# Turning expert rows in 32x32 squares on VectorE, with four first-layer banks

## The chip, the cores and the metric

The kernel runs on one core of a Trainium2 chip. Its time is device microseconds for one launch: 2286.07 us, the median of 3 runs (2285.0 to 2286.5). One more execution was profiled; it took 2288.12 us, and from its first to its last instruction (the span) 2286.2 us. All times on a trace count from the start of that span. The engines are TensorE (PE, with its weight loads PEld), VectorE (DVE), ScalarE (ACT), GpSimd (POOL) and SyncE (SP, which issues most DMAs).

## The reference

An attention without softmax, whose output goes through a mixture of experts with one expert per token.

```python
# u, v: (8, 2496, 256); z: (8, 2496, 64); f32
attn = np.maximum(z @ z.transpose(0, 2, 1) / 2496, 0.0) ** 2
x = (u * (attn @ v)).reshape(19968, 256)
logits = x @ w_gate + modality_bias[modality_id]        # 8 experts
e_idx = np.argmax(logits, axis=1)
gate = softmax(logits)[token, e_idx]
for e in range(8):                                       # w1: (8, 256, 1024), w2: (8, 1024, 256)
    h = np.maximum(x[mask_e] @ w1[e], 0.0)
    out[mask_e] = gate[mask_e, None] * (h @ w2[e])
```

## The kernel before

Matmuls are exact to f32 by parts: an operand is split into a high part, rounded to the format that PE takes (F32R), and a low part, the remainder. A product is high x high + high x low + low x high. ACT makes the high part by a copy, DVE the low part by a subtraction.

**Attention stage.** For each of 8 batches, 5 chunks of 512 queries go through 10 steps of 256 keys: scores, ReLU and square, split, and the product with v. Beside them DVE evacuates finished chunks, multiplies by u, computes the gate logits of each token (`logits`, L396, in 16 calls per chunk of two instructions of 128x256) and the routing of each batch; POOL scatters every token's row (256 values, gate, token number: 258 words) with an indirect DMA into `xs`, at the next place of its expert (`scatter`, L509). A planner (`beside`, L886) deals these pieces out over the steps by assumed costs and due steps, so it sets the order of DVE and ACT; SP's order in this stage is made by the framework's scheduler. Meanwhile the expert weights are copied to a layout of their own in DRAM, `w1s` and `w2s` (`lay_weights`, L204).

**Expert stage.** The rows of each expert are taken in tiles of 512. Tiles -4 to -1 are of the expert with most tokens so far; they run while the last batch's routing is finished (its late logits, routing, scatters and the plan of all further tiles: the list `between`, L1091 on). Tiles 0 to 34 follow by the plan, and a quarter tile of 128 rows closes (`run_quarter`, L1038). A tile (`run_tile`, L1066) has 8 passes `f`. In each, `up` (L975) makes one group of 6 matmuls over the 256 inputs for 128 hidden units into one PSUM bank `ph`, ACT takes ReLU and the high part `hh` from it, DVE the low part `hl`; two passes later `down` (L992) adds the products with w2 for the tile's four 128-row parts, into four banks `po`. After the last pass `finish` (L1004) multiplies by the gate and scatters the rows to the output. `ph` has two banks (pool `ps_h`), and two more (`ps_m`) serve all that is passing: turned rows, the last chunk's rows, the routing's counts.

The first layer contracts over the 256 inputs, so rows must be turned: inputs to partitions. `fetch` (L747) loads a tile with one DMA, four rows of 258 words per partition. `turn` (L833) has PE turn it with 8 transposes of 128x128 into two banks (`turn_rows`), and ACT and DVE take the high and the low part from there (`part_rows`). A tile turns its successor after pass 1, the tiles before 0 after pass 5; tile -4 is turned five steps before the end of attention (`turn_early`, `part_early`). `prefetch` (L1032) asks for a tile's rows up to two tiles ahead; a tile's weights are asked for two tiles ahead and split in passes 2 to 5 of the preceding tile.

Instructions of an engine run in the order given. A wait holds all behind it on that engine.

Of the kernel before, what the change touches and what calls it, by code (L numbers as in the profile page):

```python
# [9 lines left out]
F32 = mybir.dt.float32  # L10
F32R = mybir.dt.float32r
I32 = mybir.dt.int32
AF = mybir.ActivationFunctionType
ALU = mybir.AluOpType
AX = mybir.AxisListType
P = 128
T = 512
PSUM = bass.MemoryType.PSUM
# [3 lines left out]
def ins_of(x):  # L22
    return getattr(x, "ins", x)
# [3 lines left out]
def tile_attention_moe(ctx: ExitStack, tc: tile.TileContext, u, v, zt, mid, wg, mb, w1, w2, out):  # L27
# [11 lines left out]
    nc = tc.nc  # L39
    B, S, D = u.shape  # L40
# [4 lines left out]
    KD, KF = D // P, F // P  # L45
    J = T // P
# [3 lines left out]
    assert (B - 1) * S >= E * T and D == 2 * P and 2 * DK == P and LAST == T - 64 and F % P == 0  # L50
    NCOL = NCH * J
    XW = D + 2
    CAP = N
    EARLY = min(4, (B - 1) * S // E // T)
    UNC = -(-N // T) - EARLY
# [32 lines left out]
    def bank_tile(shape, name):  # L88
        return bank["pool"].tile(shape, F32, tag=bank["tag"], name=name)
# [113 lines left out]

    def lay_weights(e, n):  # L204
        if n == 0:
            nc.sync.dma_start(out=w1s[e], in_=w1[e].rearrange("(k p) f -> p k f", p=P))
        else:
            nc.sync.dma_start(out=w2s[e], in_=w2[e].rearrange("(j p) d -> p j d", p=P))

# [158 lines left out]
    def take_last_rows(b, c):  # L368
        (parts, x), ut = turned_rows.pop((b, c)), U.pop((b, c))
        for n, y in enumerate(parts):  # L370
            j = slice(n * J // 2, (n + 1) * J // 2)
            nc.vector.tensor_tensor(out=x[:, j, 0:D], in0=y, in1=ut[:, j, :], op=ALU.mult)
        X[b, c] = x
# [292 lines left out]
    def at(g, f, *args):  # L666
        tasks.setdefault(g, []).append((f, args))

    def queue(g, end, *pieces):

        due.setdefault(g, []).append((end, pieces))

    def act(us, f, *args):
        return ("A", us, f, args)

    def dve(us, f, *args):
        return ("D", us, f, args)

    def none(f, *args):
        return (None, 0.0, f, args)  # L680
# [58 lines left out]
    ready, fetched = {"n": 0}, {"n": 0}  # L739
    data = mybir.DependencyInfo(mybir.DependencyClass.Sync, mybir.DependencyReason.DATA)  # L740

    def wait_rows(i):
        for s in scatters[ready["n"]:]:
            tc.add_manual_dep(i, s.name, data, reason="rows of tokens")
        ready["n"] = len(scatters)

    def fetch(t, r0=0, nj=J):  # L747

        n = t + EARLY
        cell = first[0:1, 1:2] if t < 0 else meta[0:1, t, 0:1]  # L750
        row = nc.sync.value_load(cell, min_val=0, max_val=(E - 1) * CAP if t < 0 else E * CAP - T)
        k = fetched["n"] % 3
        fetched["n"] += 1
        xg = head[k // 2].tile([P, J, XW], F32R, tag=f"xg{k}", name="xg")[:, 0:nj, :].bitcast(F32)
        r0 += n * T if t < 0 else 0
        src = xs[bass.ds(row + r0 if r0 else row, nj * P), :]
        i = ins_of(nc.sync.dma_start(out=xg, in_=src.rearrange("(p j) c -> p j c", j=nj)))
        wait_rows(i)
        TL[t] = xg

    def weight_tiles(pool, n):
        W[n] = (
# [47 lines left out]
        if EARLY > 1:  # L810
            fetch(1 - EARLY)

    def turn_rows(t, dh):

        xg = TL[t]
        nj = xg.shape[1]
        pt = bank_tile([P, T], "pt")[:, 0:nj * P]
        for j in range(nj):
            nc.tensor.transpose(  # L819
                out=pt[:, j * P:(j + 1) * P].bitcast(F32R),  # L820
                in_=xg[:, j, dh * P:(dh + 1) * P].bitcast(F32R),
                identity=ident_r,
            )
        return pt

    def part_rows(x, dh, pt):
        nc.scalar.copy(out=x[0][:, dh, :], in_=pt)
        nc.vector.tensor_tensor(out=x[1][:, dh, :], in0=pt, in1=x[0][:, dh, :].bitcast(F32), op=ALU.subtract)

    def turned_tiles(nj):  # L830
        return [turned.tile([P, KD, T], F32R, tag="zm", bufs=NCH + 1, name=n)[:, :, 0:nj * P] for n in ("xh", "xl")]

    def turn(t):  # L833
        x = turned_tiles(TL[t].shape[1])
        for dh in range(KD):
            part_rows(x, dh, turn_rows(t, dh))
        TL[t] = (TL[t], *x)

    first_turned = []

    def turn_early(t):
        first_turned[:] = [turn_rows(t, dh) for dh in range(KD)]

    def part_early(t):
        x = turned_tiles(J)
        for dh in range(KD):
            part_rows(x, dh, first_turned[dh])
        TL[t] = (TL[t], *x)

    at(EG + 2, begin)  # L850
    for q in range(KD + 2):
        queue(G - 8 + q, G - 4 + q, act(1.05, part_weights_high, -1, q), dve(1.25, part_weights_low, -1, q))
    at(G - 5, turn_early, -EARLY)
    queue(G - 4, G - 4, none(part_early, -EARLY))

    ET = mybir.EngineType
    for c in range(3):
# [105 lines left out]
    ph1.close()  # L963

    ph2 = ctx.enter_context(ExitStack())
    ps_h = ph2.enter_context(tc.tile_pool(name="ps_h", bufs=2, space=PSUM, reuse_waits="tile"))
    bank.update(pool=ph2.enter_context(tc.tile_pool(name="ps_m", bufs=2, space=PSUM, reuse_waits="tile")), tag="m")
    mp = ph2.enter_context(tc.tile_pool(name="mp", bufs=2, reuse_waits="tile"))
    wp = ph2.enter_context(tc.tile_pool(name="wp", bufs=1, reuse_waits="tile"))
    head.append(wp)  # L970
# [31 lines left out]
    done = []  # L1002

    def finish(t, po, group):  # L1004
        xg, TL[t] = TL[t][0], None
        ids = mp.tile([P, J], I32, tag="ids", bufs=3, name="ids")[:, 0:len(po)]
        nc.vector.tensor_copy(out=ids, in_=xg[:, :, D + 1])
        mine = []
        for j in range(len(po)):
            gate = xg[:, j, D:D + 1]  # L1010
            part2 = mp.tile([P, D], F32, tag="part2", bufs=2, name="part2")
            nc.scalar.mul(out=part2, in_=po[j][:, D:2 * D], mul=gate)
            y = mp.tile([P, D], F32, tag="y", bufs=6, name="y")
            nc.vector.scalar_tensor_tensor(out=y, in0=po[j][:, 0:D], scalar=gate, in1=part2, op0=ALU.mult, op1=ALU.add)  # L1014
            i = ins_of(
                nc.gpsimd.indirect_dma_start(  # L1016
                    out=out,
                    out_offset=bass.IndirectOffsetOnAxis(ap=ids[:, j:j + 1], axis=0),
                    in_=y,
                    in_offset=None,  # L1020
                    bounds_check=N - 1,
                    oob_is_err=False,
                )
            )
            tc.declare_no_dep(i, group=group, reason="a tile's tokens are distinct")
            tc.add_to_no_dep_group(group, i)
            for s in done:
                tc.add_manual_dep(i, s.name, data, reason="rows that two tiles of an expert share")
            mine.append(i)
        done[:] = mine  # L1030

    def prefetch(t):  # L1032

        for n in range(t + 1, min(t + 3, UNC)):
            if n not in TL and (n < 0 or len(scatters) == B * NCOL):
                fetch(n)

    def run_quarter(t, part):  # L1038
# [24 lines left out]
            down(t, f, h[f], po, 0)  # L1063
        finish(t, po, f"out{t}{part}")

    def run_tile(t, ahead, extra={}, part=""):  # L1066
        if not isinstance(TL[t], tuple):
            turn(t)
        po = [ps_o.tile([P, 2 * D], F32, tag="o", name="po") for _ in range(TL[t][0].shape[1])]
        h = {}  # L1070
        for f in range(KF + 2):
            if f < KF:
                h[f] = up(t, f)
            if 2 <= f < KF:
                for j in range(len(po)):
                    down(t, f - 2, h[f - 2], po, j)
            if ahead and t >= -1 and 2 <= f < 2 + KD + 2:
                part_weights_high(t + 1, f - 2)
                part_weights_low(t + 1, f - 2)
            for g in extra.get(f, ()):  # L1080
                g()
            if f == (1 if t >= 0 else 5) and ahead and t + 1 in TL:
                turn(t + 1)
        for j in range(len(po)):
            for f in range(KF - 2, KF):
                down(t, f, h[f], po, j)
        finish(t, po, f"out{t}{part}")
# [3 lines left out]
    between = {n: {f: [] for f in range(KF + 2)} for n in range(EARLY)}  # L1091
    between[0][1] += [lambda: make_last_rows(B - 1, NCH - 1)]
    between[0][2] += [lambda: take_last_rows(B - 1, NCH - 1)]
    for n in range(LGN):
        between[0][2 + n * (KF - 2) // LGN].append(lambda n=n: logits(B - 1, NCH - 1, n))
    planning = plan()
    slots = [(n, f) for n in range(EARLY) for f in range(KF)][KF:]
    for k, pieces in ((0, (route_logits, route_exp)), (1, (route_places,)), (3, (route_count, route_slots, route_gates))):
        n, f = slots[k]
        between[n][f] += [lambda p=p: p(B - 1, LATE) for p in pieces]  # L1100
    for k, (n, f) in zip(range(LATE.start, NCOL), slots[4:]):
        between[n][f].append(lambda k=k: scatter(B - 1, k))
    for n, f in slots[5:13]:
        between[n][f].append(lambda: next(planning, None))
    n, f = slots[13]
    between[n][f] += [lambda: fetch_weights(0)]
    between[3][0] += [lambda: fetch_weights(1)]

    ph2.enter_context(tc.manual_schedule(engines={ET.PE, ET.Activation, ET.DVE, ET.Pool, ET.SP}))
    for t in range(-EARLY, UNC):  # L1110
# [63 lines left out]
```

## Time and profile before

| | us |
|---|---|
| median of 3 runs | 2286.07 (2285.0 to 2286.5) |
| the profiled execution | 2288.12 |
| its span | 2286.2 |
| PE busy | 2263.1 (99%), granted clock 0.997 |
| DVE busy | 1756.6 (77%) |
| ACT busy | 1584.1 (69%) |
| POOL busy | 364.6 (16%) |
| attention stage, to PE's first expert matmul | 1357.5 |
| expert stage, to the end | 928.7 |

Busy time says who works, not who is waited for; that is in the waits and in the chain that is followed back from the last instruction. Matmuls are shown with their pipelined length (0.39 us for 512 columns), and their starts are 0.23 us apart, so the pace of PE is read from starts.

### The profile page before, as it was taken

The page shows a single profiled execution, that of the slowest core. Times are in us where ns is not written, and L with a number is a line of the kernel's source. Part 1 is how long each engine was busy: PE and PEld are TensorE (multiplying, and loading weights), DVE is VectorE, ACT ScalarE, POOL GpSimd, SP SyncE. Part 2 cuts the span into 40 slices and gives each one's busy share as a digit, 9 for nine tenths or more (in the row PEclk, how much of TensorE's full clock was granted, in tenths as well). Part 3 has the DMA queues.
Part 4 walks back from the last instruction along what each step waited for, and adds up shares of the span by engine and source line. Part 5 has one row for each costly group of instructions (what it writes and reads, how often), then busy time and mean ns, then how long its engine had stood idle before and what let it go on. Part 6 is the DMA issues. An engine that isn't in the chain of part 4 may idle for free.

```text
span 2286.2 us, 44695 instructions
## 1 busy us (share of the span) xinstructions
PE 2263.1 (99%) x17194; PEld 1945.6 (85%) x17194; DVE 1756.6 (77%) x4544; ACT 1584.1 (69%) x1957; POOL 364.6 (16%) x349
## 2 busy tenths in 40 slices
PE   9999999999999999999999999999999999999996
PEld 7789889889899899889888888888888888888885
DVE  6889989989989889889889997555555565656563
ACT  7888888888888888888888863545444544545452
POOL 0000210210220210210210413212121212121111
PEclk9999999999999999999999999999999999999998
DMA  9612112112112112112111122434343444434340
GB/s 303 226 33 66 47 47 78 38 53 71 41 52 70 41 60 62 52 50 64 49 43 33 58 93 91 169 118 148 129 145 133 136 141 131 146 124 154 116 155 22
DMA packets 101743, 216.62 MB, mean 95 GB/s; under 512 B 15472, under 2 KB 63216, under 8 KB 96656
## 3 DMA queue, kind: packets, MB, share of 16 engines
q1 hardware_dynamic: 86432, 172.48, 23.1%
q0 software_dynamic: 15088, 41.21, 4.9%
q8 instruction: 136, 2.23, 0.4%
q14 instruction: 87, 0.71, 0.1%
HBM read 168.23 MB, written 62.19 MB: 101 GB/s over the span
## 4 chain that ended last, share of the span: by engine, by line
PE 85%; DVE 10%; issue 3%; ACT 1%; DMA 0%; POOL 0%; DVEq 0%; POOLq 0%; ACTq 0%
PE acc L305 36%; PE ph L984 18%; PE po L997 12%; PE s L265 10%; PE po L998 6%; DVE spare L403 4%; DVE al L289 3%; PE pt L819 1%; DVE vl L240 1%; DVE ah L280 1%; PE po L381 1%; DVE x L351 1%; ACT r L267 1%; ACT r L273 0%; DVE x L391 0%
## 5 line engine op out<-in xcount | busy, mean ns | idle before, releaser
L267 ACT ACTIVATE r<-s 128x1024 f32<-128x1024 f32 (+1 forms) x400 | 403.8, 1010 | 199.5 <-PE s L265 194.8
L289 DVE TENSOR_TENSOR al<-r,ah 128x1024 fp32r<-128x1024 f32 (+1 forms) x360 | 431.3, 1198 | 102.0 <-ACT ah L280 86.7
L403 DVE SCALAR_TENSOR_TENSOR spare<-x,wgb 128x256 f32<-128x256 f32 x1280 | 462.8, 423 | 1.0
L305 PE MATMUL acc<-ah,vh 64*128 64x512 f32 (+1 forms) x3120 | 454.4, 384 | 0.9 <-DVE ah L280 0.9
L997 PE MATMUL po<-w,hh 128*128 128x512 f32 x1256 | 450.1, 393 | 0.0
L988 ACT ACTIVATE hh<-ph 128x512 fp32r<-128x512 f32 x312 | 186.8, 599 | 378.3 <-PE ph L984 374.0
L305 PE MATMUL acc<-ah,vl 64*128 64x512 f32 (+1 forms) x3120 | 445.6, 383 | 0.0
L305 PE MATMUL acc<-al,vh 64*128 64x512 f32 (+1 forms) x3120 | 444.5, 382 | 0.0
L984 PE MATMUL ph<-xh,w 128*128 128x512 f32 x1248 | 439.8, 398 | 0.5 <-DVE hl L989 0.3
L273 ACT ACTIVATE r<-r 128x1024 f32<-128x1024 f32 (+1 forms) x400 | 416.8, 1042 | 3.3
L989 DVE SCALAR_TENSOR_TENSOR hl<-ph,hh 128x512 fp32r<-128x512 f32 x312 | 215.6, 691 | 248.4 <-ACT hh L988 246.9
L516 POOL DMA_INDIRECT xs<-x,sloti x160 | 204.4, 1278 | 1028.1 <-DVE x L514 946.2
L305 PEld LDWEIGHTS acc<-ah,vh 64*128 64x128 f32 x3120 | 324.0, 184 | 48.3 <-ACT x L347 2.9
L305 PEld LDWEIGHTS acc<-al,vh 64*128 64x128 f32 x3120 | 324.7, 184 | 41.8
L305 PEld LDWEIGHTS acc<-ah,vl 64*128 64x128 f32 x3120 | 319.7, 185 | 45.1
L265 PE MATMUL s<-zm 64*128 64x512 f32 (+1 forms) x2400 | 352.6, 387 | 2.3 <-ACT r L267 2.3
L998 PE MATMUL po<-w,hl 128*128 128x256 f32 x1256 | 350.7, 279 | 0.0
L280 ACT CAST ah<-r 128x1024 fp32r<-128x1024 f32 (+1 forms) x289 | 294.8, 1020 | 0.0
L997 PEld LDWEIGHTS po<-w,hh 128*128 128x128 f32 x1256 | 235.4, 187 | 56.1
L984 PEld LDWEIGHTS ph<-xh,w 128*128 128x128 f32 x1248 | 234.0, 188 | 56.9 <-DVE hl L989 2.3
L265 PEld LDWEIGHTS s<-zm 64*128 64x128 f32 x2400 | 241.7, 185 | 32.9 <-ACT r L267 4.3
L1016 POOL DMA_INDIRECT out_dram<-y,ids x157 | 153.2, 976 | 720.5 <-DVE y L1014 694.8
(152 smaller groups left out, 1975.2 us busy)
## 6 DMA issues: line engine op xcount, KB each, us to landing
w<-w1s SPq DMA_DIRECT2D x37, 1024.0 KB
w<-w2s SPq DMA_DIRECT2D x37, 1024.0 KB
xg<-xs SPq DMA_DIRECT2D x39, 516.0 KB
vr<-in_v_dram SPq DMA_DIRECT2D x32, 512.0 KB
ut<-in_u_dram SPq DMA_DIRECT2D x32, 512.0 KB
zr<-in_zt_dram SPq DMA_DIRECT2D x40, 256.0 KB
w1s<-in_moe_w_dram SPq DMA_DIRECT2D x8, 1024.0 KB
w2s<-in_moe_w_dram SPq DMA_DIRECT2D x8, 1024.0 KB
```

The lines of the kernel that those rows point to most:

```text
L265: nc.tensor.matmul(out=s[:, t, :w], lhsT=lhs, rhs=mv[halves[t], ql, :w], start=n == 0, stop=n == 2)
L267: nc.scalar.activation(out=r[:, :, :w], in_=s[:, :, :w], func=AF.Relu, scale=INV)
L273: nc.scalar.square(out=a[:, :, :w], in_=a[:, :, :w])
L280: copy(out=ah[:, :, :w], in_=st_a[g][:, :, :w])
L289: nc.vector.tensor_tensor(out=al[:, :, :w], in0=a[:, :, :w], in1=ah[:, :, :w].bitcast(F32), op=ALU.subtract)
L305: nc.tensor.matmul(out=acc[b, c][r][dh][:, :w], lhsT=V[b, k // J][y][halves[r], k % J, dh * P:(dh + 1) * P], rhs=x[halves[r], k % 2, :w], ...
L403: nc.vector.scalar_tensor_tensor(out=spare[:, k % 2, :], in0=x[:, j, 0:D], scalar=1.0, in1=wgb[:, e, :], op0=ALU.mult, op1=ALU.mult, accum ...
L516: nc.gpsimd.indirect_dma_start(out=xs, out_offset=bass.IndirectOffsetOnAxis(ap=RT[b]["sloti"][:n, k:k + 1], axis=0), in_=x[:n, j, :], in_o ...
L984: nc.tensor.matmul(out=ph, lhsT=lhs, rhs=rhs[:, k, :], start=n == 0, stop=n == 3 * KD - 1)
L989: nc.vector.scalar_tensor_tensor(out=hl, in0=ph, scalar=0.0, in1=hh.bitcast(F32), op0=ALU.max, op1=ALU.subtract)
L997: nc.tensor.matmul(out=po[j], lhsT=hh[:, s], rhs=both, start=f == 0, stop=False, skip_group_check=True)
L998: nc.tensor.matmul(out=po[j][:, 0:D], lhsT=hl[:, s], rhs=w[:, 0, :], start=False, stop=f == KF - 1, skip_group_check=True)
```

## The change

1. A fetch is now five DMAs. Four of them load 32 partitions each: partition `32 b + i` gets, for each block of 32 rows, the 64 inputs `64 b` to `64 b + 63` of row `i` of that block, in pieces of 256 bytes; the fifth loads gate and token number (`side`). A DVE `transpose` of 32x32 squares then gives `xt`, with 32 inputs of each half per group of partitions; ACT copies the high part of the whole tile, DVE subtracts the low part. PE has no transposes of expert rows any more.
2. `w1s` is laid out in the same order of inputs, with two DMAs of half the size for each expert.
3. The turn stands later: the squares after pass 6 (pass 4 in tile -3), the two parts after pass 7 (5). Tile -4 is turned by the planner from step G - 6 on.
4. `ps_h` has four banks, and all that passes takes its banks there too.
5. The last batch's late logits run two per pass from pass 2 of tile -4 on, and the routing, its scatters, the plan and the first weight fetches stand in other passes of the tiles -3 to -1; the rows of the tiles 0 and 1 are asked for in pass 2 of tile -1.

```diff
     def lay_weights(e, n):
         if n == 0:
-            nc.sync.dma_start(out=w1s[e], in_=w1[e].rearrange("(k p) f -> p k f", p=P))
+            for k in range(KD):
+                nc.sync.dma_start(
+                    out=w1s[e, :, k, :].rearrange("(b q) f -> b q f", q=BLK),
+                    in_=w1[e].rearrange("(b k q) f -> k b q f", k=KD, q=BLK)[k],
+                )
         else:
             nc.sync.dma_start(out=w2s[e], in_=w2[e].rearrange("(j p) d -> p j d", p=P))
...
         fetched["n"] += 1
-        xg = head[k // 2].tile([P, J, XW], F32R, tag=f"xg{k}", name="xg")[:, 0:nj, :].bitcast(F32)
+        words = head[k // 2].tile([P, J * XW], F32, tag=f"xg{k}", name="xg")
+        nt = nj * P
+        xg = words[:, 0:nt // BLK * KD * BLK].rearrange("p (t c) -> p t c", c=KD * BLK)
+        side = words[:, J * D:J * D + 2 * nj].rearrange("p (j c) -> p j c", c=2)
         r0 += n * T if t < 0 else 0
-        src = xs[bass.ds(row + r0 if r0 else row, nj * P), :]
-        i = ins_of(nc.sync.dma_start(out=xg, in_=src.rearrange("(p j) c -> p j c", j=nj)))
-        wait_rows(i)
-        TL[t] = xg
+        src = xs[bass.ds(row + r0 if r0 else row, nt), :]
+        dmas = []
+        for b in range(P // BLK):
+            cols = slice(b * KD * BLK, (b + 1) * KD * BLK)
+            rows_of = src[:, cols].rearrange("(t i) c -> i t c", i=BLK)
+            dmas.append(nc.sync.dma_start(out=xg[b * BLK:(b + 1) * BLK], in_=rows_of))
+        dmas.append(nc.sync.dma_start(out=side, in_=src[:, D:XW].rearrange("(j p) c -> p j c", p=P)))
+        wait_rows([ins_of(i) for i in dmas])
+        TL[t] = (side, xg)

     def weight_tiles(pool, n):
         W[n] = (
...
-    def turn_rows(t, dh):
-        xg = TL[t]
-        nj = xg.shape[1]
-        pt = bank_tile([P, T], "pt")[:, 0:nj * P]
-        for j in range(nj):
-            nc.tensor.transpose(
-                out=pt[:, j * P:(j + 1) * P].bitcast(F32R),
-                in_=xg[:, j, dh * P:(dh + 1) * P].bitcast(F32R),
-                identity=ident_r,
-            )
-        return pt
-    def part_rows(x, dh, pt):
-        nc.scalar.copy(out=x[0][:, dh, :], in_=pt)
-        nc.vector.tensor_tensor(out=x[1][:, dh, :], in0=pt, in1=x[0][:, dh, :].bitcast(F32), op=ALU.subtract)
-    def turned_tiles(nj):
-        return [turned.tile([P, KD, T], F32R, tag="zm", bufs=NCH + 1, name=n)[:, :, 0:nj * P] for n in ("xh", "xl")]
+    def turn_blocks(t):
+        side, xg = TL[t]
+        nt = xg.shape[1] * BLK
+        xt = turned.tile([P, KD, T], F32, tag="zm", bufs=NCH + 1, name="xt")[:, :, 0:nt]
+        TL[t] = (side, xt)
+        nc.vector.transpose(
+            out=xt.rearrange("p k (t i) -> p k t i", i=BLK), in_=xg.rearrange("p t (k c) -> p k t c", k=KD)
+        )
+    def part_high(t):
+        side, xt = TL[t]
+        xh, xl = (turned.tile([P, KD, T], F32R, tag="zm", bufs=NCH + 1, name=n)[:, :, 0:xt.shape[2]] for n in ("xh", "xl"))
+        nc.scalar.copy(out=xh, in_=xt)
+        TL[t] = (side, xh, xl, xt)
+    def part_low(t):
+        side, xh, xl, xt = TL[t]
+        nc.vector.tensor_tensor(out=xl, in0=xt, in1=xh.bitcast(F32), op=ALU.subtract)
+        TL[t] = (side, xh, xl)
     def turn(t):
-        x = turned_tiles(TL[t].shape[1])
-        for dh in range(KD):
-            part_rows(x, dh, turn_rows(t, dh))
-        TL[t] = (TL[t], *x)
-    first_turned = []
-    def turn_early(t):
-        first_turned[:] = [turn_rows(t, dh) for dh in range(KD)]
-    def part_early(t):
-        x = turned_tiles(J)
-        for dh in range(KD):
-            part_rows(x, dh, first_turned[dh])
-        TL[t] = (TL[t], *x)
+        for f in (turn_blocks, part_high, part_low):
+            f(t)
     at(EG + 2, begin)
     for q in range(KD + 2):
         queue(G - 8 + q, G - 4 + q, act(1.05, part_weights_high, -1, q), dve(1.25, part_weights_low, -1, q))
-    at(G - 5, turn_early, -EARLY)
-    queue(G - 4, G - 4, none(part_early, -EARLY))
+    queue(G - 6, G - 4, dve(1.2, turn_blocks, -EARLY), act(1.05, part_high, -EARLY), dve(1.25, part_low, -EARLY))
     ET = mybir.EngineType
     for c in range(3):
...
-    ps_h = ph2.enter_context(tc.tile_pool(name="ps_h", bufs=2, space=PSUM, reuse_waits="tile"))
-    bank.update(pool=ph2.enter_context(tc.tile_pool(name="ps_m", bufs=2, space=PSUM, reuse_waits="tile")), tag="m")
+    ps_h = ph2.enter_context(tc.tile_pool(name="ps_h", bufs=4, space=PSUM, reuse_waits="tile"))
+    bank.update(pool=ps_h, tag="h")
...
-        xg, TL[t] = TL[t][0], None
+        side, TL[t] = TL[t][0], None
-        nc.vector.tensor_copy(out=ids, in_=xg[:, :, D + 1])
+        nc.vector.tensor_copy(out=ids, in_=side[:, :, 1])
-            gate = xg[:, j, D:D + 1]
+            gate = side[:, j, 0:1]
...
+    def turn_at(t):
+        return 4 if t == 1 - EARLY else KF - 2
-        if not isinstance(TL[t], tuple):
+        if len(TL[t]) < 3:
...
                 g()
-            if f == (1 if t >= 0 else 5) and ahead and t + 1 in TL:
-                turn(t + 1)
+            if ahead and t + 1 in TL:
+                if f == turn_at(t):
+                    turn_blocks(t + 1)
+                if f == turn_at(t) + 1:
+                    part_high(t + 1)
+                    part_low(t + 1)
         for j in range(len(po)):
             for f in range(KF - 2, KF):
                 down(t, f, h[f], po, j)
...
+    slots = [(n, f) for n in range(EARLY) for f in range(KF)]
+    def put(slot, *pieces):
+        n, f = slots[slot]
+        between[n][f] += pieces
     for n in range(LGN):
-        between[0][2 + n * (KF - 2) // LGN].append(lambda n=n: logits(B - 1, NCH - 1, n))
+        put(2 + n // 2, lambda n=n: logits(B - 1, NCH - 1, n))
+    for slot, pieces in ((10, (route_logits, route_exp)), (11, (route_places,)), (13, (route_count,)), (14, (route_slots, route_gates))):
+        put(slot, *(lambda p=p: p(B - 1, LATE) for p in pieces))
+    for k in range(LATE.start, NCOL):
+        put(14 + k - LATE.start, lambda k=k: scatter(B - 1, k))
     planning = plan()
-    slots = [(n, f) for n in range(EARLY) for f in range(KF)][KF:]
-    for k, pieces in ((0, (route_logits, route_exp)), (1, (route_places,)), (3, (route_count, route_slots, route_gates))):
-        n, f = slots[k]
-        between[n][f] += [lambda p=p: p(B - 1, LATE) for p in pieces]
-    for k, (n, f) in zip(range(LATE.start, NCOL), slots[4:]):
-        between[n][f].append(lambda k=k: scatter(B - 1, k))
-    for n, f in slots[5:13]:
-        between[n][f].append(lambda: next(planning, None))
-    n, f = slots[13]
-    between[n][f] += [lambda: fetch_weights(0)]
-    between[3][0] += [lambda: fetch_weights(1)]
+    for slot in (15, 16, 17, 18, 18, 19, 19, 20):
+        put(slot, lambda: next(planning, None))
+    put(20, lambda: fetch_weights(0))
+    put(26, lambda: prefetch(-1), lambda: fetch_weights(1))
     ph2.enter_context(tc.manual_schedule(engines={ET.PE, ET.Activation, ET.DVE, ET.Pool, ET.SP}))
     for t in range(-EARLY, UNC):
```

The first place is DVE's queue at the end of the attention stage of the kernel before. `al` are the last low parts of attention, `w` the first expert's weights, `x<-acc` the last evacuation, `spare,lg` logits, `hl` the first low parts of tile -4.

```order
L289 TENSOR_TENSOR al<-r,ah 128x2x448
L403 SCALAR_TENSOR_TENSOR spare,lg<-x,wgb 128x256 x6
...
L403 SCALAR_TENSOR_TENSOR spare,lg<-x,wgb 128x256 x4
...
L828 TENSOR_TENSOR xl<-pt,xh 128x512 x2
...
L403 SCALAR_TENSOR_TENSOR spare,lg<-x,wgb 128x256 x6
L799 TENSOR_TENSOR w_0_18680<-w_0_18680 128x1024 x2
L403 SCALAR_TENSOR_TENSOR spare,lg<-x,wgb 128x256 x2
...
L799 TENSOR_TENSOR w_0_18681<-w_0_18681 128x4x256 x2
L351 TENSOR_TENSOR x<-acc,x 128x448 x2
...
L403 SCALAR_TENSOR_TENSOR spare,lg<-x,wgb 128x256 x2
L989 SCALAR_TENSOR_TENSOR hl<-ph,hh 128x512 x3
```

And the same stretch with the change, where `xt` are tile -4's squares.

```order
L295 TENSOR_TENSOR al<-r,ah 128x2x448
L834 STREAM_TRANSPOSE xt<-xg 128x1024
L409 SCALAR_TENSOR_TENSOR spare,lg<-x,wgb 128x256 x2
...
L409 SCALAR_TENSOR_TENSOR spare,lg<-x,wgb 128x256 x6
...
L286 CAST ah<-r 128x2x448
...
L409 SCALAR_TENSOR_TENSOR spare,lg<-x,wgb 128x256 x2
L814 TENSOR_TENSOR w_0_18688<-w_0_18688 128x1024
L846 TENSOR_TENSOR xl<-xt,xh 128x1024
...
L814 TENSOR_TENSOR w_0_18689<-w_0_18689 128x4x256 x2
L357 TENSOR_TENSOR x<-acc,x 128x448 x2
...
L409 SCALAR_TENSOR_TENSOR spare,lg<-x,wgb 128x256 x10
L991 SCALAR_TENSOR_TENSOR hl<-ph,hh 128x512 x3
```

Twenty logits stand between the first `al` shown and the first `hl` in both; ten of them are now behind the evacuation, where two were, and a transpose and a cast of `ah` are added to the queue.

The second place is DVE's queue in a steady tile of the kernel before, from the weights' last quarter over the tile's end to the next tile's passes.

```order
L799 TENSOR_TENSOR w_1_19215<-w_1_19215 128x4x256
L989 SCALAR_TENSOR_TENSOR hl<-ph,hh 128x512 x2
L1007 CAST ids<-xg 128x4
L1014 SCALAR_TENSOR_TENSOR y<-po,xg,part_20978 128x256
...
L989 SCALAR_TENSOR_TENSOR hl<-ph,hh 128x512 x2
L828 TENSOR_TENSOR xl<-pt,xh 128x512 x2
L989 SCALAR_TENSOR_TENSOR hl<-ph,hh 128x512
```

With the change, the same stretch:

```order
L814 TENSOR_TENSOR w_0_18689<-w_0_18689 128x4x256
L991 SCALAR_TENSOR_TENSOR hl<-ph,hh 128x512
L834 STREAM_TRANSPOSE xt<-xg 128x1024
L991 SCALAR_TENSOR_TENSOR hl<-ph,hh 128x512
L846 TENSOR_TENSOR xl<-xt,xh 128x1024
L1009 CAST ids<-xg 128x4
L1016 SCALAR_TENSOR_TENSOR y<-po,xg,part_20713 128x256
...
L991 SCALAR_TENSOR_TENSOR hl<-ph,hh 128x512 x3
L814 TENSOR_TENSOR w_1_19217<-w_1_19217 128x1024
```

The low part of the turned rows has moved from behind the next tile's second `hl` to behind this tile's last, and the transpose stands between the last two.

## Rows read from the trace of the kernel before

**Rows 1.** Page, busy time of each engine, share, instructions.

```profile
PE 2263.1 (99%) x17194; PEld 1945.6 (85%) x17194; DVE 1756.6 (77%) x4544; ACT 1584.1 (69%) x1957; POOL 364.6 (16%) x349
```

**Rows 2.** PE's waits: total us, times, longest.

```profile
PE s L265 <- ACT r L267: 2.3, 4, 1.1
```

**Rows 3.** Chain of waits, one expert tile: start, length, what.

```profile
1730.33 2.80 PE ph L984 x12
1733.13 0.63 PE pt L819 x8
1733.76 1.47 PE ph L984 x6
...
1753.41 2.79 PE ph L984 x12
```

**Rows 4.** PE's groups of instructions, turning matmuls: busy us, mean ns, idle before.

```profile
L819 PE MATMUL pt<-ident,xg 128*128 128x128 f32 x314 | 31.3, 242 | 0.0
```

**Rows 5.** Timeline of PE, tile -3: start, length, instruction.

```profile
1384.34 0.63 PE L984 MATMUL ph<-xh,w 128*128 128x512 f32 x2
...
1385.04 0.91 PE L984 MATMUL ph<-xh,w 128*128 128x512 f32 x2
```

**Rows 6.** Chain of waits, starts of tiles -2, -1 and 0.

```profile
1406.61 2.80 PE ph L984 x12
1429.99 2.80 PE ph L984 x12
1453.37 2.79 PE ph L984 x12
```

**Rows 7.** DVE's groups by form.

```profile
L289 DVE TENSOR_TENSOR al<-r,ah 128x1024 fp32r<-128x1024 f32 x288 | 352.6, 1224 | 75.6 <-ACT ah L280 62.9
...
L280 DVE CAST ah<-r 128x1024 fp32r<-128x1024 f32 x95 | 65.5, 690 | 4.8 <-ACT r L273 4.8
...
L280 DVE CAST ah<-r 128x896 fp32r<-128x896 f32 x16 | 9.9, 622 | 0.0
...
L462 DVE TENSOR_TENSOR_SCAN run<-reset,hot 128x160 f32<-128x160 f32 x9 | 4.4, 491 | 0.3
```

**Rows 8.** Timeline, end of a steady tile.

```profile
1721.07 1.04 ACT L795 CAST w<-w 128x1024 fp32r<-128x1024 f32 x1
...
1724.00 0.69 DVE L989 SCALAR_TENSOR_TENSOR hl<-ph,hh 128x512 fp32r<-128x512 f32 x1 [0.64 <-ACT hh L988]
...
1726.80 0.69 DVE L989 SCALAR_TENSOR_TENSOR hl<-ph,hh 128x512 fp32r<-128x512 f32 x1 [2.10 <-ACT hh L988]
...
1727.95 0.28 PE L998 MATMUL po<-w,hl 128*128 128x256 f32 x1
...
1730.40 0.39 PE L984 MATMUL ph<-xl,w 128*128 128x512 f32 x1
```

**Rows 9.** One steady tile: busy us of PE, PEld, DVE, ACT, POOL, clock, DMA.

```profile
1730.17:1753.25 23.08, 23.08 (x123) 19.44 (x122) 13.64 (x19) 11.43 (x18) 3.90 (x5) 1.00 0.42 138
```

**Rows 10.** Timeline, hand-over from attention to tile -4.

```profile
1349.47 1.29 DVE L828 TENSOR_TENSOR xl<-pt,xh 128x512 fp32r<-128x512 f32 x2
...
1361.27 1.28 DVE L989 SCALAR_TENSOR_TENSOR hl<-ph,hh 128x512 fp32r<-128x512 f32 x2
1362.00 0.19 PEld L984 LDWEIGHTS ph<-xh,w 128*128 128x128 f32 x1 [0.56 <-DVE hl L989]
```

**Rows 11.** Timeline of SP, then of POOL (tile -1, last scatter).

```profile
13.99 2.86 SPq L187 DMA_DIRECT2D mi<-in_moe_modality_id_dram  x4
...
61.56 7.94 SPq L206 DMA_DIRECT2D w1s<-in_moe_w_dram  x1
...
1430.42 1.83 SPq L757 DMA_DIRECT2D xg<-xs  x2
...
1427.50 0.91 POOL L516 DMA_INDIRECT xs<-x,sloti  x1 [1.83 <-DVE ids L1007]
```

**Rows 12.** DMA engines from 13.9 to 19.4 us.

```profile
DMA packets 4529, 0.64 MB, mean 117 GB/s; under 512 B 4333, under 2 KB 4333, under 8 KB 4528
```

More of the change, by code (lines that the diff above doesn't have):

```diff
@@ L52, in tile_attention_moe @@
     XW = D + 2
+    BLK = 32
     CAP = N
@@ L740, in tile_attention_moe, with wait_rows @@
     data = mybir.DependencyInfo(mybir.DependencyClass.Sync, mybir.DependencyReason.DATA)
-    def wait_rows(i):
+    def wait_rows(dmas):
         for s in scatters[ready["n"]:]:
-            tc.add_manual_dep(i, s.name, data, reason="rows of tokens")
+            for i in dmas:
+                tc.add_manual_dep(i, s.name, data, reason="rows of tokens")
         ready["n"] = len(scatters)
```

## The prediction

> **What bounds the kernel now.** I read the page's first part, then who TensorE (PE) waits for, then the chain of waits, and last the timeline around the places that the change touches. PE is busy for 2263.1 us of a span of 2286.2 [rows 1], and the largest of its waits on another engine adds up to 2.3 us [rows 2]: whatever leaves PE's own stream leaves the span, and whatever goes to another engine is free as long as PE doesn't begin to wait for it. In the expert stage the chain is PE alone. A tile starts at 1730.33, the next at 1753.41, so a tile takes 23.08 us [rows 3]. Twelve first-layer matmuls take 2.80 us there, then the eight turning matmuls 0.63 us, and the six matmuls behind them 1.47 us where twelve in 2.80 make 1.40 [rows 3]. Turning one tile therefore costs PE 0.63 + 0.07 = 0.70 us, and a tile without it would take 22.38 us.
>
> **What goes.** The rows count 314 turning matmuls [rows 4]: 39 tiles of 8, and 2 for the quarter tile. One tile (number -4) is turned in the attention stage, and the tiles -4 to 33 each turn their successor: 38 x 0.70 = 26.6 us. The quarter's two, by the same rows, 2 x 0.63/8 + 0.07 = 0.23 us.
>
> The first layer's result had two banks and now has four. In a tile from 0 on the turn stands between the second and the third group of first-layer matmuls and gives VectorE (DVE) the time to free the first bank. In the tiles -3 to -1 it stood later, and there the third group starts late: a pair of matmuls spans 0.91 us where others span 0.63, 0.28 too much [rows 5], and the tiles -2 and -1 take 23.38 us (1406.61 to 1429.99 to 1453.37), 0.30 over 23.08 [rows 6]. With four banks the third group takes a bank that nobody holds: 0.28 + 2 x 0.30 = 0.88 us go. Without the four banks every tile would lose this 0.3 now, since the turn no longer covers it.
>
> **What comes, in a steady tile.** DVE turns the whole tile in one instruction of 128x1024, then ScalarE (ACT) copies the high part and DVE subtracts. No row of the trace shows the transpose. From below, a copy of 128x1024 takes 0.69 us; a two-operand pass of that size takes 1.22 us; from above, the slowest streaming DVE row per element, a scan over 160 elements in 491 ns, is 3.07 ns each, 3.14 us for 1024 [rows 7]. I take 1.2 us, the row of one element per lane and step. The Trainium skill has a price (page Vector Engine (DVE) Microarchitecture Reference, section 3.8 on the reshape front-end: the array sustains one element per cycle per lane); with the 0.96 GHz of VectorE: DVE Perf Modes that is an estimate of 1.07 us plus a start, and by it the sum would stay as below. No run here shows it yet.
>
> Where does it lie? At the end of a steady tile, DVE ends the low part of group 6 at 1724.69 (1724.00 + 0.69) and begins that of group 7 at 1726.80; the transpose goes between them, and the second layer needs the latter, 0.69 us long, at 1727.95 [rows 8]. So it may last 1727.95 - 0.69 - 1724.69 = 2.57 us, some 2.5 with the hand-on between engines, before PE waits; 1.2 fits twice. ACT has ended group 7 when DVE begins it, at 1726.80; it copies the high part in 1.04 us, as long as it takes for a quarter of the weights, to 1727.84; DVE subtracts in 1.2 us to 1729.1, and PE wants this low part with the next tile's second matmul, at 1730.40: 1.3 us spare [rows 8]. The output products that queue behind the subtraction come a few tenths later, and their banks are next wanted two groups into the next tile. Cost: 0. DVE is busy for 13.64 us of a tile [rows 9], so 1.1 us more is room it has.
>
> The rule that speaks against the change is in VectorE: DVE Perf Modes (Trainium skill, rules for kernel authors): turn 128x128 on TensorE if PSUM can take it, VectorE has only 32x32. Here the rows agree that TensorE is quick (88 ns for each of eight), but it is the engine without a gap, and the blocks need no further step, since the loads place the squares; by the rule the time would stay at 2286, by the rows it falls.
>
> **What comes, at the hand-over from attention.** DVE works through here: its queue up to the first low part of tile -4 decides when PE can start that tile's third group, which waited 0.33 us for it until 1362.00 [rows 10]. The order of the queue shows 20 logits before it in both kernels (ten of them now stand behind the last evacuation, two before), plus the transpose, 1.2 us, plus a cast of 128x896 that was ACT's, 0.62 us [rows 7], and one subtraction of 1.22 us for two that took 1.29 [rows 7, 10]. The low part comes 1.2 + 0.62 - 0.07 = 1.75 us later. Banks don't help: this tile's first two groups and the two banks of the last rows fill all four, so the third group still takes the first bank. PE starts it at 1363.75, and the 0.7 us that the turn in the attention stage gave back is lost in that wait. Cost 1.75. In the rest of tile -4 DVE has four logits, 1.4 us, in each pass beside the low part, the transpose and the subtraction; placed one after the other, the subtraction ends as PE wants it: 0.1 us.
>
> **Routing, plan, weights.** They run two passes later on DVE and POOL in the tiles -3 and -2, which have room with the logits thinner. Tile 0's rows are asked for in pass 2 of tile -1, after the last scatter; before, the request followed the last scatter (1427.50) by 2.9 us [rows 11]; that is now about 7.5 us into the tile, and the turn comes 18 us in. The five loads of a fetch hold SP longer: four loads of small pieces took it 2.86 us, 0.72 each, so at most 3.6 us [rows 11]; behind them stand the weights, wanted a tile later. Cost: 0.
>
> **Sum.** 26.60 + 0.23 + 0.88 - 1.75 - 0.10 = 25.9 us. The profiled execution took 2288.12 us, of which 1.9 lie around the span; it becomes 2262.2. The median of the runs shown is 2.05 below it, and the forecast is put against that: 2286.07 - 25.9 = 2260.2, say 2260. With the transpose at 0.69 us the hand-over costs 0.5 less (2259.7); at 3.14 us it costs 1.9 more, and each of 38 tiles waits 0.64 us, 24.3 us: 2286.5, the gain gone.
>
> **Rivals.**
> (a) The transpose is slow and PE waits for group 7's low part in each tile. From 2.5 us on it costs 38 times the excess, from 2.5 + 25.9/38 = 3.2 us on the kernel is slower. If squares are read with four passes at the two-operand rate, 4.9 us: 2.4 x 38 = 91 and 3.7 at the hand-over, 2355. For it: four strided dimensions, no such row. Against: both ends write and read runs of 32 words, and even filling and emptying the squares one after the other, 2.4 us, stays under the limit. 0.05; between 3.0 and 3.2 us, no change, 0.03.
> (b) The loads in the attention stage come late. The expert weights, laid out in the first 80 us before, now stand in SP's order among the loads of the first five batches, w1 in two halves; one such row held SP for 7.94 us [rows 11]. Against: these loads run up to three buffers ahead. At 0.5 us for each of the 16 halves, 8 us: 2268. 0.09.
> (c) Rows of 256 bytes land late: a fetch is 2560 pieces for 128. In 5.5 us the DMA engines moved 4333 packets under 512 bytes [rows 12], so a fetch needs 3 to 4 us of them, and the share in a tile was 0.42 [rows 9]. A fetch has 39 us from the start of one tile to pass 6 of the next; only tile 0 has little, 10 us, and a wait there is paid once: 2265. DMA: Bandwidth & Descriptors (Trainium skill, specifications) asks for 512 bytes, below which a piece is read and written back; even twice the time would end inside both slacks, and no run here shows it. 0.04.
>
> **How the numbers follow.** Forecast 0.79 (2256 to 2265: the hand-over from nothing to 4 us, the attention stage's few stalls gone or new), (b) 0.09, (c) 0.04, (a) 0.08. The range 2256 to 2268 takes in the first three, and leaves out a transpose past 2.7 us. Within 0.2% of 2286, which is about what a measurement can tell from no change, lies the flat part of (a): 0.03; slower, its long part: 0.05; faster 0.92.
>
> **What would show it.** Right: tiles 22.4 us apart with no wait of PE between them, the transpose near 1.2 us, a wait of some 3 us of PE for the low part once, in the third group of tile -4, and attention that ends where it did, within 1 us. Wrong: a wait of PE in every tile for the low part of group 7 or for the turned rows (a), PE waiting in batches 1 to 4 behind ACT and a load (b), or the transpose of tile 0 waiting for a DMA (c). A period other than 22.4 without any wait would say that the 0.07 us beside the turn, or the matmuls' own pace, were misread.

## The result and the profile after

The changed kernel takes 2262.57 us (median of 4 runs, 2260.78 to 2263.76) against 2286.28 for the kernel before (2285.0 to 2286.74): a ratio of 0.9897, 95% interval 0.9879 to 0.9914. The forecast was 2260, with a range of 2256 to 2268. The profiled execution took 2263.76 us; its span is 2261.6, 24.6 shorter than that of before.

The page's first part, busy time and share of each engine, answers to [rows 1]:

```profile
PE 2235.1 (99%) x16880; PEld 1924.5 (85%) x16880; DVE 1800.4 (80%) x4545; ACT 1579.3 (70%) x1916; POOL 365.7 (16%) x349
```

PE has 314 instructions fewer, the turning matmuls of [rows 4], and 28.0 us less to do. DVE has 43.8 us more. The groups by form, DVE (busy us, mean ns | idle before):

```profile
L834 DVE STREAM_TRANSPOSE xt<-xg 128x1024 f32<-128x1024 f32 x39 | 48.2, 1236 | 0.0
L846 DVE TENSOR_TENSOR xl<-xt,xh 128x1024 fp32r<-128x1024 f32 x39 | 47.8, 1225 | 9.3 <-ACT xh L841 9.3
```

The transpose takes 1.24 us. Its idle time of 0.0 says that none of the 39 ever waited for a load. The timeline of PE gives the starts of two successive tiles, to be held against [rows 3]:

```profile
1720.64 0.40 PE L986 MATMUL ph<-xh,w 128*128 128x512 f32 x1
1720.88 0.39 PE L986 MATMUL ph<-xl,w 128*128 128x512 f32 x1
...
1743.02 0.40 PE L986 MATMUL ph<-xh,w 128*128 128x512 f32 x1
```

Tiles are 22.38 us apart. DVE in the tile's end ahead of 1720.64 answers to [rows 8] (a bracket holds the idle time before and what ended it):

```profile
1714.47 0.69 DVE L991 SCALAR_TENSOR_TENSOR hl<-ph,hh 128x512 fp32r<-128x512 f32 x1 [0.64 <-ACT hh L990]
1715.08 1.23 DVE L834 STREAM_TRANSPOSE xt<-xg 128x1024 f32<-128x1024 f32 x1
1717.27 0.69 DVE L991 SCALAR_TENSOR_TENSOR hl<-ph,hh 128x512 fp32r<-128x512 f32 x1 [0.95 <-ACT hh L990]
1718.20 1.23 DVE L846 TENSOR_TENSOR xl<-xt,xh 128x1024 fp32r<-128x1024 f32 x1 [0.24 <-ACT xh L841]
```

After the transpose DVE is idle for 0.95 us, where it was idle for 2.10 without it [rows 8]. The low part ends at 1719.43, and PE takes it at 1720.88: 1.45 us to spare. PE's waits on other engines, with total, number and longest:

```profile
PE ph L986 <- DVE hl L991: 3.1, 1, 3.1
PE s L271 <- ACT r L273: 2.3, 4, 1.1
```

Only the first is new. It is the hand-over, and DVE's queue ahead of it, against [rows 10], ends:

```profile
1357.88 0.42 DVE L409 SCALAR_TENSOR_TENSOR spare<-x,wgb 128x256 f32<-128x256 f32 x1
...
1361.06 0.41 DVE L409 SCALAR_TENSOR_TENSOR spare<-x,wgb 128x256 f32<-128x256 f32 x1
...
1361.41 1.28 DVE L991 SCALAR_TENSOR_TENSOR hl<-ph,hh 128x512 fp32r<-128x512 f32 x2
```

Ten logits stand between the last evacuation and the low part. PE, free since 1359.05, starts the third group at 1362.14:

```profile
1362.14 0.79 PE L986 MATMUL ph<-xh,w 128*128 128x512 f32 x1 [3.10 <-DVE hl L991]
```

What follows was not foreseen: the stretches from the wait on (busy us of PE, PEld, DVE, ACT, POOL, then PE's granted clock, the DMA share and GB/s) show the clock at 0.50 from 1362 to 1368 us, the lower of its two levels (1.2 and 2.4 GHz).

```profile
1360.00:1362.00 2.00, 0.00 (x0) 0.00 (x0) 2.00 (x11) 0.00 (x0) 0.00 (x0) 0.84 0.06 21
1362.00:1364.00 2.00, 1.86 (x4) 1.49 (x5) 0.69 (x2) 0.00 (x0) 0.00 (x0) 0.50 0.93 191
1364.00:1366.00 2.00, 2.00 (x7) 1.60 (x6) 0.27 (x1) 0.60 (x1) 0.00 (x0) 0.50 0.75 74
1366.00:1368.00 2.00, 2.00 (x8) 1.71 (x7) 2.00 (x6) 0.00 (x0) 0.00 (x0) 0.50 0.00 0
1368.00:1370.00 2.00, 2.00 (x11) 1.67 (x10) 1.00 (x6) 0.60 (x1) 0.00 (x0) 0.95 0.00 0
```

One view misleads here. The chain of waits of before followed PE through the tiles; that of after runs through the scatters of the output:

```profile
1683.33 14.23 issue
...
1701.62 4.51 DMA out_dram<-y,ids
1706.20 13.74 issue
```

A chain is followed back from the last instruction to what released it, and here it has found the queue of scatters, each behind the one before. PE has no idle time over 0.05 us from 1362.14 to the end of its last matmul at 2243.75, so PE still sets the time; a 14 us "issue" in a chain says that the view has lost its thread.

Where the 24.6 us of the two spans lie, from the starts of the tiles in both timelines:

| stretch | before | after | difference |
|---|---|---|---|
| start to tile -4 | 1357.48 | 1354.77 | -2.71 |
| tile -4 | 24.99 | 29.81 | +4.82 |
| tile -3 | 23.98 | 22.74 | -1.24 |
| tiles -2 and -1 | 46.76 | 44.76 | -2.00 |
| tiles 0 to 34 | 807.38 | 783.30 | -24.08 |
| quarter tile and end | 25.61 | 26.22 | +0.61 |

### The profile page after: what moved, and what is told of

It reads as the page before. It is cut to its first block, busy times and chain, and to the rows that moved or that the text cites. A ratio compares the mean times of both kernels' runs of the same rounds, so it can differ in the third digit from the quotient of the medians.

```text
span 2261.6 us, 44421 instructions
## 1 busy us (share of the span) xinstructions
PE 2235.1 (99%) x16880; PEld 1924.5 (85%) x16880; DVE 1800.4 (80%) x4545; ACT 1579.3 (70%) x1916; POOL 365.7 (16%) x349
## 4 chain that ended last, share of the span: by engine, by line
PE 51%; issue 28%; DVE 9%; DMA 6%; POOL 3%; ACT 1%; SPq 0%; POOLq 0%; DVEq 0%; ACTq 0%
PE acc L311 37%; PE s L271 10%; DMA out_dram<-y,ids 6%; POOL out_dram L1018 3%; DVE spare L409 3%; DVE al L295 2%; PE ph L986 1%; PE po L999 1%; DVE vl L246 1%; PE po L387 1%; DVE ah L286 1%; DVE x L357 1%; ACT r L273 1%; PE po L1000 1%; ACT r L279 0%
## 5 line engine op out<-in xcount | busy, mean ns | idle before, releaser
L986 PE MATMUL ph<-xh,w 128*128 128x512 f32 x1248 | 431.8, 397 | 3.1 <-DVE hl L991 3.1
```

What stands on the lines that cost most here:

```text
L986: nc.tensor.matmul(out=ph, lhsT=lhs, rhs=rhs[:, k, :], start=n == 0, stop=n == 3 * KD - 1)
```

## The experiments

Each stands against runs of the kernel before on the same chip; the changed kernel stood at 0.9897 of it.

**Four banks alone undone.**

```diff
-    ps_h = ...tile_pool(name="ps_h", bufs=4, ...)
-    bank.update(pool=ps_h, tag="h")
+    ps_h = ...tile_pool(name="ps_h", bufs=2, ...)
+    bank.update(pool=...tile_pool(name="ps_m", bufs=2, ...), tag="m")
```

> The changed kernel, but the first layer has two banks and what passes has two of its own, as before the change. Theory (the turn no longer covers the third group, so two banks cost every tile the 0.30 us seen in the tiles -2 and -1 of the kernel before): 39 tiles x 0.30 = 11.7 us more than the changed kernel, about 2274 us, tiles 22.68 us apart, and in each a pair of first-layer matmuls of the third group that spans 0.91 us where others span 0.63. Rival (with the turn gone from PE the first bank is free in time, and the four banks are worth nothing): 2262.6 us, tiles 22.38 us apart.

Measured: 2272.16 us, ratio 0.9934 (0.9918 to 0.9951). Tiles are 22.66 apart, and in PE's timeline the third group's first pairs are late, as in [rows 5]:

```profile
1723.49 0.63 PE L986 MATMUL ph<-xh,w 128*128 128x512 f32 x2
...
1724.19 0.92 PE L986 MATMUL ph<-xh,w 128*128 128x512 f32 x2
```

The banks are worth 0.28 us per tile, 11 us of the gain that the turn alone would have lost again. The two spans differ by only 7.6 us, since tile -4 is 2.74 us shorter here than in the profile of after and begins 0.91 sooner. And the same wait of 3.10 us at the hand-over (1358.13 to 1361.23) left the clock alone:

```profile
1360.00:1362.00 2.00, 0.77 (x3) 0.67 (x4) 1.77 (x6) 0.00 (x0) 0.00 (x0) 1.00 0.37 79
1362.00:1364.00 2.00, 2.00 (x11) 1.67 (x10) 0.44 (x1) 0.60 (x1) 0.00 (x0) 1.00 1.28 181
```

So the low clock follows that wait in some executions and not in others.

**Ten logits taken out of the hand-over.** The planner's last logits go behind the low parts, dealt out with the late ones.

```diff
+        behind = [p[0][3] for _, _, p in waiting if p[0][2] is logits]
+        waiting = [q for q in waiting if q[2][0][2] is not logits]
...
-    for n in range(LGN):
-        put(2 + n // 2, lambda n=n: logits(B - 1, NCH - 1, n))
+    pieces = behind + [(B - 1, NCH - 1, n) for n in range(LGN)]
+    for slot, n in zip(range(1, 10), (2, 2, 3, 3, 3, 2, 2, 2, 2)):
+        for _ in range(n):
+            put(slot, lambda p=pieces.pop(0): logits(*p))
```

> The changed kernel, but the five calls of logits (ten instructions, 3.5 us of DVE) that stand ahead of tile -4's first low part stand behind its second, and the 21 late calls are dealt two or three to a pass from pass 1 to pass 9. Theory (DVE's queue makes PE wait 3.10 us at the hand-over, and the granted clock of 0.50 behind it, from 1362 to 1368 us, follows from that wait): the wait of 3.10 us goes, and the slow 6.1 us take some 2.7 us less, 5.8 us in all: 2256.8 us, clock 1.00 throughout. Rival 1 (the low clock comes from something else there, as the loads at 1362 to 1364 us with a DMA share of 0.93): only the wait goes, 2259.5 us, the clock still at 0.50. Rival 2 (the logits only move the wait into the next passes, where DVE is then late): 2261 to 2264 us, waits of PE for hl or the turned rows in tile -4.

Measured: 2257.01 us (2255.46 to 2259.09), ratio 0.9869 (0.9852 to 0.9885). Its slowest run lies under the changed kernel's fastest, 2260.78, though the intervals of the two ratios overlap. DVE's queue and PE's third group at the hand-over:

```profile
1357.67 1.32 DVE L994 SCALAR_TENSOR_TENSOR hl<-ph,hh 128x512 fp32r<-128x512 f32 x2
1358.91 0.41 DVE L409 SCALAR_TENSOR_TENSOR spare<-x,wgb 128x256 f32<-128x256 f32 x1
```

```profile
1358.59 0.49 PE L989 MATMUL ph<-xh,w 128*128 128x512 f32 x1
```

PE no longer waits for DVE in the expert stage, the clock is 1.00 in every stretch from 1352 to 1370 us, and tile -4 takes 23.73 us for 29.81. The two profiles show that the wait of 3.10 us went with the logits. That the low clock was its consequence fits them, and the medians, which lie 5.6 us apart, but one profile can't show it: the clock also stayed at 1.00 in three of the five profiles that have the wait. It fell in none of the five that don't. The loads alone don't bring it: their share was 1.07 at 1362 to 1364 us here, with the clock at 1.00.

**Squares turned twice and three times.** In each tile after -4:

```diff
+        for _ in range(2 if t > -EARLY else 1):     # 3 in the second kernel
             nc.vector.transpose(...)
```

> The changed kernel, but DVE turns the squares of each tile after -4 twice over (the second time gives the same result): 1.2 us more of DVE per tile at the place of the transpose. Theory (2.5 us lie free there; the two take 2.4): no change, 2262.6 us within 2, tiles 22.38 us apart. Rival (DVE's work at the end of a tile already counts): up to 38 x 1.2 = 46 us more, 2308 us.

> The changed kernel, but DVE turns the squares of each tile after -4 three times over. Theory (a limit at 2.5 us between group 6's low part and group 7's): three take 3.6 us, 1.1 too many in each of 38 tiles, 42 us more, 2304 us, tiles 23.5 us apart, with a wait of PE for the low part of group 7 in each. Rival 1 (the slack is larger, since banks and products behind it can wait): 2262.6 us. Rival 2 (the turned rows, not group 7, are late as well): over 2310 us, with a second wait of PE at the tile's second matmul.

Twice: 2263.51 us, ratio 0.9894 (0.9878 to 0.9911), tiles 22.38 to 22.42 apart; 1.2 us more of DVE cost nothing. Only the tiles -4 and -3, where logits and routing fill DVE, wait for it, 1.03 and 0.39 us. Three times: 2311.14 us, ratio 1.0102 (1.0085 to 1.0119), slower than before, and 7 us above the 2304 expected. Its chain shows the three and what waits (start, length):

```profile
1689.36 1.25 DVE xt L835
1690.63 1.26 DVE xt L835
1691.91 1.25 DVE xt L835
1693.15 0.59 DVE hl L992
1693.78 0.39 PE po L1001
```

and PE's waits (total, number, longest) hold one in each of 38 tiles:

```profile
PE po L1001 <- DVE hl L992: 37.3, 38, 2.3
```

Tiles are 23.58 apart, 1.20 more. With 3.72 us for three, the limit lies at 3.72 - 1.20 = 2.5 us, where the prediction put it; two transposes, 2.48 us, lie just under it and cost nothing. The wait itself is 0.93 in most tiles, but waits are counted from the end of a pipelined matmul, and the pace is read from starts:

```profile
1692.46 0.39 PE L1000 MATMUL po<-w,hh 128*128 128x512 f32 x1
1693.78 0.39 PE L1001 MATMUL po<-w,hl 128*128 128x256 f32 x1 [0.93 <-DVE hl L992]
1694.00 0.40 PE L1000 MATMUL po<-w,hh 128*128 128x512 f32 x1
```

These starts are 1.32 and 0.22 us apart, where 0.23 and 0.12 are usual: 1.19 us, all of the loss at this one place. The time is the one that rival 2 had named, but its second wait, for the turned rows, did not come up. What the expectation had too small was the three transposes, 3.72 us and not 3.6, which makes 0.1 in each tile, and the tiles -4 and -3, where logits fill DVE: they lost 4.10 and 1.82 us.

**Banks and routing without the squares.** The kernel before with four banks and the new passes:

```diff
-    ps_h = ...tile_pool(name="ps_h", bufs=2, ...)
+    ps_h = ...tile_pool(name="ps_h", bufs=4, ...)
+    bank.update(pool=ps_h, tag="h")
...
+    for n in range(LGN):
+        put(2 + n // 2, lambda n=n: logits(B - 1, NCH - 1, n))
...
```

> The kernel before with two parts of the change alone: the four banks, and the last batch's logits, routing, plan and weights in their new passes. TensorE still turns the rows, at the old places, from rows loaded as before. Theory (the turn itself carries the gain): the tiles -3 to -1 lose their 0.28 to 0.30 us, 0.9 us in all, and tiles stay 23.08 us apart: ratio to the kernel before 0.9996, some 2285 to 2287 us. Rival (banks and routing carry a good part of it): 2275 us or less, with tiles closer than 23.08 us.

Measured: 2285.04 us, ratio 0.9993 (0.9983 to 1.0002), which is not told from no change. The chain still has the turn in every tile:

```profile
1519.52 2.80 PE ph L984 x12
1522.32 0.63 PE pt L819 x8
1522.95 1.47 PE ph L984 x6
...
1542.60 2.79 PE ph L984 x12
```

Tiles are 23.08 us apart, as before, and the tiles -3 to -1 together are 1.2 us shorter. So nearly all of the gain needs the turn, and the run with two banks shows what the banks keep of it. Whether the new passes of the routing are needed for it, no run shows.

**The turn early in the tile.**

```diff
     def turn_at(t):
-        return 4 if t == 1 - EARLY else KF - 2
+        return 4 if t == 1 - EARLY else KF - 2 if t < 0 else 1
```

> The changed kernel, but from tile 0 on the squares are turned after pass 1 and the two parts taken after pass 2, beside the weights' parts, in place of pass 6 and 7. Theory (DVE has idle time in every pass, and two groups lie between a low part and its use): DVE falls 0.3 us behind in pass 2 and makes it up, no wait of PE, 2262.6 us within 2, tiles 22.38 us apart. Rival (DVE's weights parts and the turn collide, which is why the change put it late): a wait of PE of 0.3 us or more for hl in every tile from 0 on, 2272 us or more.

Measured: 2262.24 us, ratio 0.9893 (0.9877 to 0.9910), tiles 22.38 apart. DVE from pass 1 on:

```profile
1701.38 1.23 DVE L834 STREAM_TRANSPOSE xt<-xg 128x1024 f32<-128x1024 f32 x1
1702.54 0.65 DVE L991 SCALAR_TENSOR_TENSOR hl<-ph,hh 128x512 fp32r<-128x512 f32 x1
1703.11 1.21 DVE L814 TENSOR_TENSOR w<-w 128x1024 fp32r<-128x1024 f32 x1
1704.24 1.22 DVE L846 TENSOR_TENSOR xl<-xt,xh 128x1024 fp32r<-128x1024 f32 x1
1705.38 0.68 DVE L991 SCALAR_TENSOR_TENSOR hl<-ph,hh 128x512 fp32r<-128x512 f32 x1
```

DVE has no idle time here for over 5 us and PE doesn't notice. Late in the tile is one good place, not the only one.

**The loads of small pieces made twice.**

```diff
-        for b in range(P // BLK):
+        for b in list(range(P // BLK)) * 2:
```

> The changed kernel, but each of the four loads of 256-byte pieces of a fetch is made twice over: 2560 pieces more per tile. Theory (a fetch has a tile and more to land, and SP and the DMA engines have room): no change, 2262.6 us within 2; the transposes never wait for a load. Rival (the small pieces are near a limit of the DMA engines, or SP's queue holds the weights' loads up): PE waits for turned rows or for weights in each tile, 2270 us or more.

Measured: 2261.04 us, ratio 0.9890 (0.9873 to 0.9906). In a steady tile the DMA share (last column but one) rises from 0.47 to 0.59, first the changed kernel:

```profile
1720.50:1742.90 22.40, 22.40 (x113) 18.78 (x112) 14.74 (x19) 11.39 (x18) 3.91 (x5) 1.00 0.47 142
```

```profile
1720.50:1742.90 22.40, 22.40 (x114) 18.79 (x113) 14.74 (x19) 11.38 (x17) 3.92 (x5) 1.00 0.59 165
```

One of the transposes waited for a load, for 1.0 us, off PE's path. The four loads take 0.12 x 22.4 = 2.7 us of the 16 DMA engines; (c) had 3 to 4 for a fetch. At the hand-over the scatters ran late, and PE waited 2.01 us for POOL and 0.81 for DVE instead of 3.10 for DVE.

**The kernel before once more.** No edit.

> The kernel before, unchanged, profiled once more, for the first 20 us. If the granted clock of 0.66 from 10 to 15 us belongs to this kernel, it is there again and the attention's scores reach the same step 1.7 us later than in the changed kernel; if it came from that one execution, the clock is 1.00 there and the span is shorter by some 1 to 2 us, 2284 to 2285 us.

Measured: 2288.04 us, span 2286.1. The clock from 10 to 15 us was low again; the same stretch of the changed kernel's profile stands below it:

```profile
10.00:15.00 5.00, 4.70 (x28) 3.78 (x30) 4.29 (x6) 3.54 (x5) 0.00 (x0) 0.66 1.00 398
```

```profile
10.00:15.00 5.00, 4.85 (x40) 3.68 (x42) 4.30 (x6) 4.15 (x6) 0.00 (x0) 1.00 1.01 409
```

But it doesn't belong to this kernel: it was 0.66 in both profiles of before, in that of the turn early and that of the doubled loads, and 1.00 in the other six, among them the kernel before with the new banks. From PE's first wait on ACT, at 6.3 to 7.6 us, to a step at some 218 us it takes 211.6 to 211.7 us in the six and 212.8 to 212.9 in the four: 1.2 us, which falls to either kernel. It is not without order: the four are those in which that first wait began latest, at 7.31 to 7.59 us, against 6.30 to 7.17 in the six. No run tested whether that is the reason. The first wait itself came 0.4 us sooner in the profile of after than in that of before, 1.7 in all.

## Why the prediction was right, and what it missed

**The turn.** Forecast 0.70 us per tile and a tile of 22.38; measured 22.38. The tiles 0 to 34 gave 24.08, for 34 x 0.70 + 0.23 = 24.03 in the sum.

**The banks.** Forecast 0.88 in the tiles -3 to -1 beside their 0.70; the three gave 3.24, 0.26 more than 3 x 0.70 + 0.88 = 2.98. Without the banks each tile would lose 0.3, it said; 0.28 by the run with two banks.

**The transpose.** Taken at 1.2 us, by the row of one element per lane and step: 1.24. So (a) fell, and the limit from which it would have come true, 2.5 us, was found by turning two and three times. The estimate of 1.07 us plus a start that the prediction drew from the Trainium skill (Vector Engine (DVE) Microarchitecture Reference, section 3.8) agrees with the 1.24 of the trace, if the start is 0.17. The Trainium skill's rule to turn 128x128 on TensorE (VectorE: DVE Perf Modes, rules for kernel authors) did not hold for this kernel: TensorE had no idle time, VectorE had, and the kernel that turns on VectorE took 2262.57 us for 2286.28.

**The hand-over.** The queue was read rightly: PE's third group was to start 1.75 us later, and 1362.14 lies 0.14 behind 1362.00 although the attention ahead of it runs 1.71 earlier in the profile of after: 1.85 later. The step that failed is the price, "Cost 1.75". It counted only the wait. In this execution the clock fell behind it, and from the third group to the tile's end PE took 22.44 us for 20.47 before, which still held the turn: 22.44 - (20.47 - 0.70) = 2.67 us more. The kernel that turns early in the tile has the same instructions in this stretch and the same wait ahead of it; with the clock at 1.00 it takes 19.70 us, 2.74 less. Of the five profiles with a wait of 3.09 or 3.10 us there, two show it (the changed kernel and the one that turns three times), three don't. The wait began at 1358.86 and 1359.04 us in the two, at 1358.08, 1358.13 and 1360.66 in the three. What decides between them is open.

**Attention, routing, rows.** From the step at 17 to 19 us to one at 1320 us both kernels take the same, 1303.1 us, so the moved weight loads cost nothing, and (b) fell. The rows of tile 0 were asked for 9.7 us into tile -1, not 7.5, and held SP for 2.5 us instead of at most 3.6; no transpose waited, so (c) fell.

**Beside the sum.** The start, clock and loads, gave 1.7 us to the profile of after and the quarter tile's end took 0.6 (from PE's last matmul to the end of the span it was 15.8 to 18.1 us over ten profiles). 25.9 + 1.7 - 2.67 - 0.6, with 0.3 from the tiles -3 to -1, is 24.6, the difference of the spans. By the medians the change is worth 23.7 us. That it stops 2.2 short of the forecast is of the size of the clock's part, which some executions pay and some don't; which of the timed ones did is not shown. In the profiled execution the hand-over cost 1.85 + 2.67 = 4.5 us, more than the 4 that the forecast's likeliest case allowed; the range of 2256 to 2268 held because it had room for other causes, which did not come.

## What to carry to other kernels

When one engine has no gap, read the time of a move from that engine's own stream, and check the receiver at the one place where its slack is smallest: how long its next wait for someone else is, and what its result is needed for. A resource that another step's time covered (here the first bank) must be looked for when that step goes. A hand-over between stages is where such a receiver has no slack, and work that nobody needs yet should not stand in its queue there.

## What the hardware showed beside this

TensorE's granted clock was 0.50 for about 6 us behind an idle time of 3.1 us, in two of five executions. It was 0.66 over 10 to 15 us in four of ten, behind the idle times of 1.12 and 0.85 us between 6 and 11 us that every execution has. The same instructions thus take 2.7 or 1.2 us more in some executions.
